# Attention over summed memory slots, then a channel mix: q turned on VectorE in 32x32 blocks of bf16 pairs, scores in 32x32 array tiles, steps in a new order

## The chip, the cores and the metric

The kernel runs on one core of a Trainium2 chip. The metric is the device time of one execution in microseconds (us). Five engines run side by side, each with its own instruction queue worked off in order: PE (TensorE: matmuls; PEld is its weight load), DVE (VectorE), ACT (ScalarE), POOL (GpSimd), SP (SyncE, which here issues DMAs). PE, DVE and ACT compute; the 16 DMA engines move data between HBM and the on-chip memory SBUF. Matmuls write PSUM, eight banks, which DVE and ACT read.

## The reference

Eight batches, eight heads, 576 tokens, 64 dims, 32 memory slots; then a channel mix over the 8 x 576 = 4608 tokens of 512 channels with a hidden width of 1024:

```python
a = exp(phi - max_s phi); a = a / sum_s a            # phi: [B, H, 576, 32]
k_m = einsum('bhsm,bhsd->bhmd', a, k)                # 32 x 64 for each head
v_m = einsum('bhsm,bhsd->bhmd', a, v)
attn = softmax_m(q @ k_m^T / 8)                      # [B, H, 576, 32]
x = attn @ v_m                                       # heads side by side: [B, 576, 512]
x_prev = x shifted by one token, zeros first
xk = mu_k * x + (1 - mu_k) * x_prev;  xr = mu_r * x + (1 - mu_r) * x_prev
out = sigmoid(xr @ w_r) * (relu(xk @ w_k) ** 2 @ w_v)
```

## The kernel before, in words

All loads cast to bf16 on their way in. Rows are read as `(a p j)`: four groups a, 128 partitions p, nine tokens j in each partition. So group a holds two heads, the even one in partitions 0 to 63 and the odd one in 64 to 127, and 64 partitions hold one head's 576 tokens as nine blocks of 64 (QR = 64). Inside the kernel a batch's tokens stand in an order of its own (JT: even j first, then odd j), cut in two halves of 320 and 256 tokens; the stores put them back.

For each batch b the function `attention(b)` offers steps by name, and the list PLAN at the head of the file says in which order they are recorded. Every engine works its own instructions off in that order, so PLAN is the schedule of all queues: `b:step` is a step of batch b, `p:` a load of the start, `c`n`:`i the hidden columns i of token chunk n, `g:`t the gate and `o:`t the output of token tile t (128 tokens, 36 of them).

The steps of a batch, in the order of its data:

- `load` (L291): four DMAs of POOL (phi, k, v, q of batch b+2), 576 KB each.
- `exp` (L224) on ACT; `z` (L243), nine matmuls that sum it, and a reciprocal on DVE; `kv` or `k`, `v` (L227), 72 matmuls each.
- `nk` (L268), `tk` (L295): k_m normalised on DVE, turned by PE, copied to `kmT` by DVE.
- `q0`, `q1` (L332), in batch 0 `qh0`, `qh1` (L319): q is turned to dims x tokens by 18 PE transposes for each, into PSUM, and copied to `qT` by DVE (in batches 0 and 1 half of it by ACT). In batches 5, 6 and 7 `qx` (L313) does it instead, with two DMA transposes that SP issues. `hold` (L263) is a small POOL copy of batch 5's `qT`, behind which the loads of the last two batches stand.
- `s0`, `s1` (L347): the scores of the even and of the odd heads, eight matmuls each in 64x32 tiles of the array (64 dims deep, 32 slots wide), then two exponentials on ACT.
- `l0` to `l3` (L365), `r0z` and its like, `w0` and its like: the softmax's sum by a matmul, its logarithm and reciprocal on ACT, the product on DVE (in batches 0 and 1 by halves, `h0z`, `y0`).
- `x0`, `x1` (L392), `dd` (L406), `k0d`, `r0d` and their like (L417): attn @ v_m, the difference to the token before, and xk and xr, by ACT and DVE. In batches 0 and 1 `mk`, `mr` (L437) do this in matmuls instead: for each half a first set of eight for the tokens themselves and one more set for each run of tokens before them, then four copies out of PSUM, two on ACT and two on DVE.

The channel mix is `c`n (`key`, L514: four matmuls, ReLU on ACT, square on DVE), `g` (`gate`, L537: four matmuls, exponential on ACT, and at every odd tile the two activations over 1024 columns that finish the sigmoid of two tiles) and `o` (`value`, L554: eight matmuls, product on DVE, `store`). `store` (L496) issues one DMA for each block of 64 tokens that a tile touches. All PSUM tiles come from one pool of eight banks in turn. `busy4` (L191) is four matmuls on zeros while batch 0's softmax runs.

Of the kernel before, what the change touches and what calls it, by code (L numbers as in the profile page):

```python
# [11 lines left out]
BF16 = mybir.dt.bfloat16  # L12
AF = mybir.ActivationFunctionType
# [5 lines left out]
    "p:q:0a 0:exp1 0:exp0 0:z 0:k0c p:q:0b 0:hn0 0:qh0 0:ht0 0:qh1 p:k:0b 0:s0 0:mub p:v:0a 0:l0 0:k1c 0:l1 0:hn1",  # L19
    "p:v:0b 0:mu 0:ht1 p:wr:0-4 0:h1z 0:v0c 0:s1 0:v1c p:phi:1 0:h0z 0:y1 0:l2 0:l3 0:nk0 0:y0 0:nk1 0:h3z 0:nr1",  # L20
    "p:wk:4-8 0:h2z 0:busy4 0:nr0 0:y3 0:y2 0:mr1 0:mr0 p:wk:0-4 0:mk1 1:exp g:2 g:0 0:mk0 g:3 1:z c0:2a c0:7b c0:6b",
    "c0:4a c0:1b p:k:1 p:q:1 c0:2b 1:k 1:nk c0:0b c0:7a c0:5b c0:3a c0:1a 1:q0 c0:3b 1:q1 1:tk c0:4b c0:0a 1:s0 p:v:1",
    "1:s1 1:v c0:6a 1:l1 1:nr1 1:l0 c0:5a p:wv:0-2 1:nk0 1:l2 p:wv:2-4 1:nk1 1:nr0 1:h1z 1:l3 0:load 1:y1 1:h2z 1:h0z",
    "1:h3z g:1 1:y3 o:3a o:2a 1:y2 1:y0 o:2b o:3b 1:mk1 o:1b 1:mk0 1:mr0 c1:5 1:mr1 c1:2 2:exp c1:6 c1:3 c1:1 c1:0",
    "1:load 2:z g:4 g:5 2:q1 2:q0 2:kv 2:nk o:0b 2:load o:1a 2:tk 3:exp 2:nv c1:7 2:s1 2:s0 c1:4 2:l2 o:0a 2:l1 3:z",
    "2:l0 2:r0z 2:w0 2:l3 2:r1z 2:w1 o:4 o:5 2:x0 3:kv 3:nk 3:nv g:6 3:tk 3:q0 3:q1 2:x1 2:dd 2:k0d g:7 g:8 3:s0",
    "2:k2d 3:s1 o:6 o:7 3:l0 2:r2d 3:l2 3:load 3:l1 2:r0d 3:l3 3:r1z c2:3 4:exp c2:2 c2:5 3:r0z 3:w1 c2:0 3:w0 c2:4",
    "c2:6 g:10 c2:1 4:z 3:x1 4:kv 4:nk 4:nv c2:7 3:x0 g:11 3:dd 4:q0 4:q1 4:tk 5:exp o:11 g:9 5:qx o:10 5:z 5:kv",
    "3:k0d 4:s1 3:k2d 4:s0 o:9 g:12 4:l3 5:nk 3:r0d 4:l2 c3:2 c3:6 5:nv 4:l0 4:l1 4:r1z 4:w1 c3:3 4:r0z 4:w0 5:tk",
    "c3:7 c3:4 3:r2d c3:0 c3:5 5:s0 5:hold 5:load 4:x1 o:8 c3:1 5:l1 4:x0 4:dd g:13 4:k2d 5:l0 g:14 o:13 4:load o:12",  # L30
    "7:exp 5:r0z 4:k0d g:16 5:w0 g:15 7:z 7:kv 5:s1 c4:5 7:qx c4:1 c4:4 6:qx 4:r0d 7:nv c4:0 c4:3 6:exp 5:l2 7:nk",
    "5:l3 c4:6 c4:2 c4:7 5:r1z 5:w1 4:r2d g:17 o:15 o:16 7:tk 5:x0 o:17 6:z 5:x1 6:kv 6:nk 7:s0 6:nv g:18 6:tk 5:dd",
    "5:k0d g:19 5:k2d o:18 o:14 6:s0 6:s1 c5:6 c5:0 6:l3 5:r0d 6:l2 6:l0 6:l1 c5:2 c5:5 6:r0z c5:7 c5:3 6:r1z 6:w1",
    "7:l0 6:w0 c5:1 g:20 7:l1 c5:4 7:s1 6:x1 5:r2d o:19 7:r0z 6:x0 6:dd 6:k2d 7:l3 g:22 6:k0d 7:w0 g:21 7:l2 g:23",
    "7:r1z o:20 o:21 7:w1 o:23 6:r2d c6:0 c6:6 c6:4 g:26 c6:1 c6:5 7:x1 c6:3 6:r0d c6:2 c6:7 7:x0 7:dd o:22 g:24 g:27",
    "7:k2d 7:k0d g:25 o:25 o:26 7:r2d o:24 c7:5 g:30 c8:6 c7:0 c7:2 c7:1 c8:1 o:27 c8:4 c7:7 6:load 7:r0d c7:3 c7:6",
    "c7:4 c8:2 c8:7 g:28 g:29 c8:3 c8:0 c8:5 g:31 o:28 o:29 o:31 7:load g:32 o:30 g:33 g:34 g:35 o:32 o:33 o:34 o:35",
]

LOADS = {None: ("phi", "k", "v", "q"), 2: ("phi", "k", "q", "v")}  # L40
# [4 lines left out]
NJ = 9  # L45
JT = (0, 2, 4, 6, 8, 1, 3, 5, 7)
# [3 lines left out]
def kernel(  # L50
# [24 lines left out]
    HALVES = (slice(0, 5 * QR), slice(5 * QR, S))  # L75
# [135 lines left out]
    def attention(b):  # L211
# [51 lines left out]
        def hold():  # L263

            spare = work.tile([1, 2], BF16, name="spare", tag="spare", bufs=1)
            nc.gpsimd.tensor_copy(spare, st["qT"][0:1, :, 0, 0])

        def norm_k(cs=(0, 1)):  # L268

            def go():  # L270
                if "kbd" not in st:
                    st["kbd"] = work.tile([128, 2, 2, D], BF16, name="kbd", tag="kbd", bufs=3)
                for c in cs:
                    nc.vector.tensor_scalar_mul(
                        st["kbd"][:, c], st["k"][c].unsqueeze(1).to_broadcast([128, 2, D]), st["rz"][:, c:c + 1])
            return go
# [18 lines left out]
        def tr_k(cs=(0, 1)):  # L295

            def go():
                n = len(cs)
                ps = ps_tile([128, n, 128], BF16, "ktps")
                for i, c in enumerate(cs):  # L300
                    nc.tensor.matmul(ps[:, i], lhsT=st["kbd"][:, c].rearrange("p h d -> p (h d)"), rhs=identity,
                                     is_transpose=True, start=True, stop=True, skip_group_check=True)
                if "kmT" not in st:
                    st["kmT"] = work.tile([128, 2, 128], BF16, name="kmT", tag="kmT", bufs=3)
                nc.vector.tensor_copy(st["kmT"][:, cs[0]:cs[0] + n], ps)
            return go

        def q_tile():
            if "qT" not in st:
                st["qT"] = work.tile([128, 2, HH * NJ // 2, QR], BF16, name="qT", tag="qT", bufs=3)  # L310
            return st["qT"]

        def cross_q():  # L313
            for hg in range(2):
                nc.sync.dma_start_transpose(out=q_tile()[:, hg],
                                            in_=qs[b % 2][ROWS[hg]].rearrange("p n d -> p (n d)"))

        def tr_q_rows(hg):

            def go():  # L320
                r = ROWS[hg]
                for i in range(2):
                    ps = ps_tile([128, NJ, QR], BF16, "qtps")
                    for n in range(NJ):
                        n0 = 2 * (NJ * i + n)
                        nc.tensor.matmul(ps[:, n], rhs=identity[r, r], is_transpose=True,  # L326
                                         lhsT=qs[b % 2][r, n0:n0 + 2, :].rearrange("p n d -> p (n d)"),
                                         start=True, stop=True, skip_group_check=True)
                    (nc.scalar.copy if i else nc.vector.tensor_copy)(q_tile()[:, hg, NJ * i:NJ * (i + 1)], ps)
            return go  # L330

        def tr_q(i):  # L332
            def go():
                pss = [ps_tile([128, NJ, QR], BF16, "qtps") for _ in range(2)]
                for n in range(NJ):
                    n0 = 2 * (NJ * i + n)
                    for hg in range(2):
                        r = ROWS[hg]
                        nc.tensor.matmul(pss[hg][:, n], rhs=identity[r, r], is_transpose=True,  # L339
                                         lhsT=qs[b % 2][r, n0:n0 + 2, :].rearrange("p n d -> p (n d)"),  # L340
                                         start=True, stop=True, skip_group_check=True)
                for hg in range(2):
                    (nc.scalar.copy if b < 2 and hg else nc.vector.tensor_copy)(
                        q_tile()[:, hg, NJ * i:NJ * (i + 1)], pss[hg])
            return go

        def scores(c):  # L347

            def go():
                if "e" not in st:  # L350
                    st["e"] = work.tile([128, 2, S], BF16, name="e", tag="e", bufs=3)
                pss = [half_tile(hf, "scps") for hf in range(2)]
                for g in (0, 2, 1, 3):
                    m = slice(g * M, (g + 1) * M)
                    for hf in range(2):
                        n = [NJ * g + j for j in JT[5 * hf:5 + 4 * hf]]
                        r = ROWS[n[0] % 2]
                        nc.tensor.matmul(pss[hf][m, :], lhsT=st["kmT"][r, c, m],  # L358
                                         rhs=st["qT"][r, c, n[0] // 2:n[-1] // 2 + 1].rearrange("p j t -> p (j t)"),
                                         start=True, stop=True, skip_group_check=True)  # L360
                for hf in range(2):
                    nc.scalar.activation(st["e"][:, c, HALVES[hf]], pss[hf], AF.Exp, scale=scale)  # L362
# [41 lines left out]
        before = [[(QR, 5 * QR, 5 * QR), (1, QR, 4 * QR)], [(5 * QR, S, 0)]]  # L404

        def diff(pr, n=1):  # L406

            def go():
# [3 lines left out]
                for lo, hi, p0 in before[1] + before[0]:  # L412
                    nc.vector.tensor_sub(d[:, :, lo:hi], x[:, :, lo:hi], x[:, :, p0:p0 + hi - lo])  # L413
# [23 lines left out]
        def mixed(w, hf):  # L437

            def go():
# [7 lines left out]
                for i in range(ND):  # L447
# [6 lines left out]
                 "z": esum, "nk": norm_k(), "nv": norm_v, "tk": tr_k(), "load": reload, "mu": load_mu, "mub": load_mu_b, "qx": cross_q,  # L454
                 "zr": sum_rows, "hold": hold}
        for i in range(2):
            steps[f"q{i}"] = tr_q(i)
            steps[f"qh{i}"] = tr_q_rows(i)
# [16 lines left out]
        for i in range(2):  # L475
            steps[f"s{i}"] = scores(i)
# [19 lines left out]
    def store(o, t, cols):  # L496
        g = t * 128
        eng = nc.sync
        while g < (t + 1) * 128:
            b, r = divmod(g, S)  # L500
            p = g - t * 128
            j, p0 = divmod(r, QR)
            n = min(QR - p0, (t + 1) * 128 - g)
# [117 lines left out]
```

## Time and profile before

| | us |
|---|---|
| median of 3 runs (lowest, highest) | 209.13 (207.54, 209.47) |
| the profiled execution | 208.79 |
| span of its instructions | 207.0 |
| PE busy, DVE busy, ACT busy in it | 192.7, 133.9, 159.4 |
| first matmul, last matmul's product | 5.93, 203.23 |
| software DMA queue (the loads) | 20.91 MB |

The profile gives, for one execution, the busy time of each engine, the chain of work that ended last, and the groups of equal instructions. The span starts with the first instruction; 1.8 us of the execution's time lie around it. A "start to start" time below is the distance between the first instruction of a piece of work on PE and the first of the next piece: since matmuls are pipelined, it is what the piece costs PE, and the busy time of a row is more.

### The profile page before, as it was taken

The numbers are of one execution on the slowest core, as the hardware profiler recorded it, in microseconds if no ns is written. First come the engines' busy times: TensorE is split into PE (matmuls) and PEld (weight loads), VectorE is DVE, ScalarE is ACT, GpSimd is POOL, SyncE is SP. The second block draws the span as 40 slices with busy tenths as digits, with TensorE's granted clock in tenths as the row PEclk, the third lists the DMA queues.
The fourth block names the chain that finished last, engine by engine and source line by source line (L and its number), as shares of the span: only waits on it lengthen the run. The fifth ranks groups of instructions, "written<-read, shape, count | busy, mean of one in ns | idle before, by whom it ended". The sixth has DMA issues, their size and how long they took to land.

```text
span 207.0 us, 5511 instructions
## 1 busy us (share of the span) xinstructions
PE 192.7 (93%) x2213; PEld 103.6 (50%) x2235; DVE 133.9 (65%) x360; ACT 159.4 (77%) x314; POOL 29.6 (14%) x46
## 2 busy tenths in 40 slices
PE   0489999999999999999999999999999999999992
PEld 0355577745655445544458654444444444444441
DVE  1236455884668996899594969767887856615232
ACT  3246999987968998979899977899968655686570
POOL 7644222201504000007400000000000000000000
PEclk9999999999999999999999999999999999999999
DMA  6999999999999999298999997832060215202525
GB/s 160 178 208 260 207 207 205 261 221 292 209 284 240 262 269 201 61 133 205 187 231 298 198 165 115 189 71 52 0 152 5 51 33 119 54 0 62 135 67 141
DMA packets 31641, 33.06 MB, mean 160 GB/s; under 512 B 9072, under 2 KB 26752, under 8 KB 31616
## 3 DMA queue, kind: packets, MB, share of 16 engines
q0 software_dynamic: 17392, 20.91, 54.2%
q1 hardware_dynamic: 13456, 10.96, 24.5%
q10 hardware_dynamic: 768, 0.85, 1.3%
q8 instruction: 17, 0.28, 0.5%
q14 instruction: 8, 0.07, 0.1%
HBM read 38.28 MB, written 9.44 MB: 231 GB/s over the span
## 4 chain that ended last, share of the span: by engine, by line
PE 89%; DMA 6%; issue 1%; POOL 1%; ACT 1%; DVE 0%; SPq 0%; POOLq 0%; DVEq 0%
PE pk L520 31%; PE pv L565 29%; PE pr L543 15%; DMA q<-in_q_dram 4%; PE kvps L237 3%; PE zps L372 2%; PE mxps L288 2%; DMA qT<-q 2%; PE scps L358 2%; PE nops L288 2%; PE qtps L339 1%; PE idle L195 1%; PE zps L247 1%; PE mub L200 1%; PE qtps L326 1%
## 5 line engine op out<-in xcount | busy, mean ns | idle before, releaser
L520 PE MATMUL pk<-xkT,wk 128*128 128x512 bf16 (+4 forms) x346 | 66.9, 340 | 0.4
L565 PE MATMUL pv<-wv,sq 128*128 128x512 bf16 (+1 forms) x322 | 65.6, 353 | 0.4
L524 ACT ACTIVATE rl<-pk 128x512 bf16<-128x512 f32 (+3 forms) x80 | 41.9, 560 | 9.9 <-PE pk L520 8.7
L528 DVE TENSOR_TENSOR sq<-rl 128x512 bf16<-128x512 bf16 (+5 forms) x104 | 32.3, 340 | 26.0 <-ACT rl L524 25.0
L565 PEld LDWEIGHTS <-sq 128*128 128x128 bf16 x328 | 31.4, 98 | 30.0 <-issue 0.5
L520 PEld LDWEIGHTS <-wk 128*128 128x128 bf16 x352 | 32.9, 98 | 26.5 <-issue 0.5
L567 DVE TENSOR_TENSOR o<-sg,pv 128x512 f32<-128x512 f32 (+1 forms) x41 | 24.9, 619 | 18.9 <-PE pv L565 14.1
L543 PE MATMUL pr<-wr,xrT 128*128 128x512 bf16 x134 | 34.6, 381 | 0.5
L548 ACT ACTIVATE sg<-pr 128x512 f32<-128x512 f32 x36 | 21.3, 611 | 12.3 <-PE pr L543 5.2
L543 PEld LDWEIGHTS <-xrT 128*128 128x128 bf16 x144 | 13.5, 98 | 15.4 <-ACT xrT L449 0.4
L550 ACT ACTIVATE sg<-sg 128x1024 f32<-128x1024 f32 x18 | 19.0, 1057 | 0.6
L551 ACT ACTIVATE sg<-sg 128x1024 f32<-128x1024 f32 x18 | 19.0, 1057 | 0.6
L401 ACT CAST x<-nops 128x320 bf16<-128x320 f32 (+1 forms) x48 | 15.8, 428 | 3.6 <-PE nops L288 3.6
L423 DVE TENSOR_SCALAR mu_d<-diff,mu 128x576 bf16<-128x576 bf16 x48 | 15.5, 364 | 0.1
L389 DVE TENSOR_TENSOR atn<-e,lz 128x576 bf16<-128x576 bf16 (+2 forms) x20 | 12.4, 635 | 4.0 <-ACT lz L382 3.8
L377 ACT ACTIVATE lz<-zps 128x320 f32<-128x320 f32 (+1 forms) x32 | 11.9, 420 | 1.6 <-PE zps L372 1.6
L362 ACT ACTIVATE e<-scps 128x320 bf16<-128x320 f32 (+1 forms) x32 | 11.0, 416 | 1.5 <-PE scps L358 1.5
L382 ACT ACTIVATE lz<-lz 128x576 f32<-128x576 f32 (+2 forms) x20 | 11.6, 600 | 0.2
L413 DVE TENSOR_TENSOR diff<-x 128x1024 bf16<-128x1024 bf16 (+1 forms) x18 | 9.0, 554 | 3.4 <-ACT x L401 3.4
L225 ACT ACTIVATE em<-ph 128x1152 bf16<-128x1152 f32 (+1 forms) x9 | 9.4, 1050 | 2.1 <-DMA ph<-in_phi_dram 2.1
L237 PE MATMUL kvps<-kv,em 64*32 64x128 bf16 (+1 forms) x720 | 9.3, 219 | 1.0 <-DMA kv<-in_k_dram 1.0
L424 DVE TENSOR_TENSOR xkT<-x,mu_d 128x1152 bf16<-128x1152 bf16 x12 | 9.1, 759 | 0.4
(66 smaller groups left out, 140.7 us busy)
## 6 DMA issues: line engine op xcount, KB each, us to landing
out_dram<-o SPq DMA_DIRECT2D x61, 128.0 KB, 2.4
ph<-in_phi_dram POOLq DMA_DIRECT2D x7, 576.0 KB, 20.8
kv<-in_k_dram POOLq DMA_DIRECT2D x7, 576.0 KB, 17.3
q<-in_q_dram POOLq DMA_DIRECT2D x7, 576.0 KB, 21.3
kv<-in_v_dram POOLq DMA_DIRECT2D x7, 576.0 KB, 18.8
out_dram<-o SPq DMA_DIRECT2D x18, 64.0 KB, 5.6
wk<-in_moe_w_k_dram POOLq DMA_DIRECT2D x2, 512.0 KB, 14.7
wv<-in_moe_w_v_dram POOLq DMA_DIRECT2D x2, 512.0 KB, 20.0
```

Source lines behind the costliest of these rows:

```text
L237: nc.tensor.matmul(kvps[c][g * M:(g + 1) * M], lhsT=em[ROWS[c], j, g, :], rhs=kv5[ROWS[c], parts, g, j, :], start=j == 0, stop=j == NJ - 1 ...
L401: nc.scalar.copy(st["x"][:, i, sl], pss[i])
L423: nc.vector.tensor_scalar_mul(t[:, i], st["d"][:, pr + i, :], mu1[:, o:o + 1])
L520: nc.tensor.matmul(pk[:, p0 - lo:p1 - lo], lhsT=wk_sb[:, di, fi * 128:(fi + 1) * 128], rhs=xk_T[:, di, p0 % RING:p0 % RING + p1 - p0], sta ...
L524: nc.scalar.activation(rl, pk, AF.Relu)
L528: nc.vector.tensor_mul(sq[:, fi, p:p + p1 - p0], rl[:, p0 - lo:p1 - lo], rl[:, p0 - lo:p1 - lo])
L543: nc.tensor.matmul(pr, lhsT=xr_T[:, di, c0:c0 + 128], rhs=wr_sb[:, di, :], start=(di == 0), stop=(di == ND - 1))
L548: nc.scalar.activation(sg[:, t % 2], pr, AF.Exp, scale=-1.0)
L550: nc.scalar.activation(sg, sg, AF.Ln, bias=1.0)
L551: nc.scalar.activation(sg, sg, AF.Exp, scale=-1.0)
L565: nc.tensor.matmul(pv[:, cols], lhsT=sq[:, fi, p:p + 128], rhs=wv_sb[:, fi, cols], start=(fi == 0), stop=(fi == NF - 1))
L567: nc.vector.tensor_mul(o[:, cols], gated[t // 2][:, t % 2, cols], pv[:, cols])
```

## The change

- q is turned by DVE alone: `turn_q` views the bf16 pairs of q as 32-bit words and transposes them in 32x32 blocks. A block of 32 tokens by 64 dims comes out as 32 dim pairs by 32 tokens, the two dims of a pair side by side. The PE transposes, the copies, the DMA transposes (`qx`) and `hold` are gone.
- The scores follow that layout: 32 dims at a time, first the even and then the odd ones, accumulated in PSUM; 16 matmuls of 288 tokens for `s0` or `s1`, and from batch 1 on one step `s` of 32 with four PSUM tiles. `rhs` takes every second bf16 of `qT`. `kbd` and `kmT` are laid out for it (`nk`, `tk`).
- Tokens stand in two halves of 288, each nine blocks of 32 (PB). `mk`, `mr` of the second half take four sets instead of two; `dd` is two subtractions over both halves at once, one of a single token and the copy of the first token (four instructions, as before). A store covers up to four blocks in one DMA (two in the last two tiles).
- `settle`: the two activations that finish a gate are a step of their own (`sg`).
- `busy4` is gone; batch 2 loads v before q; PLAN is another order throughout. The matmuls, loads and element counts of all other steps are as they were.

```diff
-    "p:q:0a 0:exp1 0:exp0 0:z 0:k0c p:q:0b 0:hn0 0:qh0 0:ht0 0:qh1 p:k:0b 0:s0 0:mub p:v:0a 0:l0 0:k1c 0:l1 0:hn1",
-    "p:v:0b 0:mu 0:ht1 p:wr:0-4 0:h1z 0:v0c 0:s1 0:v1c p:phi:1 0:h0z 0:y1 0:l2 0:l3 0:nk0 0:y0 0:nk1 0:h3z 0:nr1",
-    "p:wk:4-8 0:h2z 0:busy4 0:nr0 0:y3 0:y2 0:mr1 0:mr0 p:wk:0-4 0:mk1 1:exp g:2 g:0 0:mk0 g:3 1:z c0:2a c0:7b c0:6b",
...
+    "p:q:0a 0:exp0 0:exp1 0:z 0:mub 0:k0c p:k:0b 0:qh0 0:k1c 0:hn0 0:ht0 0:s0 p:q:0b 0:hn1 0:l0 0:h0z 0:qh1 0:ht1",
+    "0:y0 p:v:0b 0:v1c 0:l1 0:nr1 p:v:0a 0:s1 p:wr:0-4 0:nk1 0:v0c 0:nr0 0:h1z 0:l2 0:h2z 0:nk0 p:wk:4-8 0:y1 0:mu",
+    "0:y2 0:l3 0:h3z 0:y3 p:phi:1 0:mk0 0:mr1 0:mr0 0:mk1 g:2 c0:6a c0:7a 1:exp p:wk:0-4 c0:5b g:3 c0:2a g:1 c0:0a",
...
-LOADS = {None: ("phi", "k", "v", "q"), 2: ("phi", "k", "q", "v")}
+LOADS = {None: ("phi", "k", "v", "q")}
...
-    HALVES = (slice(0, 5 * QR), slice(5 * QR, S))
+    HS = S // 2
+    PB = 32
+    HALVES = (slice(0, HS), slice(HS, S))
...
+        def turn_q(rows_, gs):
+            def go():
+                dst = q_tile()[rows_, gs].rearrange("p g n h -> p (g n h)")
+                src = qs[b % 2][rows_, gs.start * NJ:gs.stop * NJ].rearrange("p n d -> p (n d)")
+                nc.vector.transpose(dst.bitcast(U32), src.bitcast(U32))
+            return go
...
-                pss = [half_tile(hf, "scps") for hf in range(2)]
-                for g in (0, 2, 1, 3):
+                pss = {(c, hf): half_tile(hf, "scps") for c in cs for hf in range(2)}
+                for h in range(2):
+                    for g in range(HH):
+                        m = slice(g * M, (g + 1) * M)
+                        for c in cs:
+                            for hf in range(2):
+                                r = slice((2 * c + hf) * PB, (2 * c + hf + 1) * PB)
+                                nc.tensor.matmul(pss[c, hf][m, :], lhsT=st["kmT"][r, h, m], rhs=st["qT"][r, g, :, h],
+                                                 start=h == 0, stop=h == 1, skip_group_check=True)
...
-        before = [[(QR, 5 * QR, 5 * QR), (1, QR, 4 * QR)], [(5 * QR, S, 0)]]
+        before = [[(PB, HS, 0), (1, PB, HS - PB)], [(HS + PB, S, HS), (HS + 1, HS + PB, S - PB), (HS, HS + 1, HS - 1)]]
...
-            steps[f"q{i}"] = tr_q(i)
-            steps[f"qh{i}"] = tr_q_rows(i)
+            steps[f"q{i}"] = turn_q(slice(0, 128), slice(2 * i, 2 * i + 2))
+            steps[f"qh{i}"] = turn_q(ROWS[i], slice(0, HH))
...
-            j, p0 = divmod(r, QR)
-            n = min(QR - p0, (t + 1) * 128 - g)
-            dst = out[b].rearrange("(p j) d -> p j d", j=NJ)[p0:p0 + n, JT[j], cols]
-            eng.dma_start(out=dst, in_=o[p:p + n, cols])
+            hf, r = divmod(r, HS)
+            j = r // PB
+            n = min(NJ - j, ((t + 1) * 128 - g) // PB, 2 if t >= NTOK // 128 - 2 else 4)
+            dst = out[b].rearrange("(h p j) d -> h j p d", h=2, j=NJ)[hf, j:j + n, :, cols]
+            eng.dma_start(out=dst, in_=o[p:p + n * PB, cols])
...
-            if t % 2 == 1:
-                nc.scalar.activation(sg, sg, AF.Ln, bias=1.0)
-                nc.scalar.activation(sg, sg, AF.Exp, scale=-1.0)
+    def settle(p):
+        def go():
+            nc.scalar.activation(gated[p], gated[p], AF.Ln, bias=1.0)
+            nc.scalar.activation(gated[p], gated[p], AF.Exp, scale=-1.0)
+        return go
```

## The prediction

> **What bounds the kernel now.** I read the page's busy shares first, then the chain, then one window for the body, then the waits. From the page:
>
> ```profile
> PE 192.7 (93%) x2213; PEld 103.6 (50%) x2235; DVE 133.9 (65%) x360; ACT 159.4 (77%) x314; POOL 29.6 (14%) x46
> ...
> DMA  6999999999999999298999997832060215202525
> ...
> PE 89%; DMA 6%; issue 1%; POOL 1%; ACT 1%; DVE 0%; SPq 0%; POOLq 0%; DVEq 0%
> ```
>
> From the first softmaxes on, PE is the bound, as the window from the first `mixed` matmul to the last product shows (columns: PE, PEld, DVE, ACT, POOL busy):
>
> ```profile
> 19.11:203.20 184.09, 182.36 (x1996) 97.05 (x2017) 126.92 (x331) 151.28 (x297) 18.15 (x25) 1.00 0.79 156
> ```
>
> PE idles 1.7 us in 184.1. The one data wait of that stretch in PE's list of waits is batch 6's q, turned by DMA:
>
> ```profile
> PE scps L358 <- DMA qT<-q: 0.4, 1, 0.4
> ```
>
> The DMA row says something else: until slice 16 (83 us) it stands at 9. The loads run without a pause; in 20 to 40 us:
>
> ```profile
> DMA  9999999999999999999999999999999999999999
> ...
> q0 software_dynamic: 4693, 4.33, 126.0%
> ...
> ```
>
> 4.33 MB in 20 us is 0.217 MB/us, so a load that casts (576 KB, 0.59 MB) takes 2.7 us, and phi, which is read at the width it keeps, about half, 1.4. Asked window by window, the loads' queue has moved 13.75 MB by 71 us and 16.17 by 84; added up in the order of the loads, q of batch 4 ends at 13.83 MB, 71 us, ahead of its use at 81.2, and q of batch 5 at 16.19 MB, 84 us. Batch 1's q lands at 30.5 (a POOL load waits for its slot till then) and is used at 31.2. So loads are just ahead of PE, and nothing but spare room on the DMA engines keeps them there.
>
> **The change part by part.** Sums are against the profiled execution, 208.79 (span 207.0, 1.8 around it); the median of the three runs is 209.13, 0.3 above.
>
> *The turn of q, PE.* A turn's start to start on PE is read from the timeline (start, us):
>
> ```profile
> 50.79 0.70 PE L339 MATMUL qtps<-identity,q 64*128 64x64 bf16 x36
> 51.42 0.80 PE L237 MATMUL kvps<-kv,em 64*32 64x128 bf16 x72
> ...
> 54.98 0.46 PE L358 MATMUL scps<-qT,kmT 64*32 64x320 bf16 x16
> 55.38 1.04 PE L520 MATMUL pk<-xkT,wk 128*128 128x512 bf16 x4
> ```
>
> 0.63 for a batch; batches 2 to 4 three times that, batch 1 0.37 twice: 2.63 us leave PE. Batch 6's wait for the DMA turn goes too, 0.45. What is late next there is the turn on DVE.
>
> *The turn of q, DVE.* No row shows this operation. 576 four-byte words a partition: below lies the 450 ns of the copy of 576 bf16 (L343), above twice a 512-word float product (L567, 684 ns), 1.37 us. Nearest is one pass at the product's rate, 684 x 576/512 = 0.77. Fourteen of these (batch 0: two of 1.4) replace fourteen copies of 0.45: DVE goes from 126.9 to some 131 us of 184, so it stays under PE. Batch 0's two turns stand in the chain of the start; there `k0b` takes q's landing slot (11.0) and q's second half k's (12.7). Turn to 14.1, scores at 15.0 (before 15.7), first `mixed` matmul at 18.2 (before 19.1); the 16 PSUM tiles of its four steps, emptied by two engines at 0.44 each, push the first gate to 21.4 (21.34 before), with 0.48 of `mixed` already done. I take -0.4; between -1.2 and +1.0. `mub` and `busy4` lay in waits and cost nothing either way.
>
> *Scores.* Sixteen matmuls for both heads' parity cost 0.40 (above), eight cost 0.28 (108.46 to 108.74): a second round of eight tiles adds 0.12. The new step has 32 in two rounds of 16 tiles. If all 16 run together, 0.40; if eight do, as the rows show, 0.28 + 3 x 0.12 = 0.64; if every second element also halves the rate, 1.1. I take 0.45, nearest to the two rounds, since 72 kvps matmuls in 0.73 us show 10 ns from one to the next, 0.32 for 32. Today's seven batches cost about 3.2 (two are split in 0.28 + 0.28): 7 x 0.45 = 3.15, no change; -0.4 to +4.5.
>
> The Trainium skill, "TensorE: Matmul & The Clock Gate", section "Wait — 56ns, not 53.3ns?", says that starts never come closer than some 25 ns; by it the 32 would take 0.8 and the seven batches 2.4 us more. The kvps row (10 ns) speaks against it.
>
> *`mixed`.* Sixteen matmuls take 0.36 (40.70 to 41.06) and 24 take 0.47, so a set of eight short ones 0.12; batch 1 has four sets more, +0.44; batch 0's are in the start. New waits of the new order: +0.5 (0 to 3). ACT, `nk`, `dd` and `settle` keep their element counts beside PE's 182 us of work. POOL loses `hold`, so the last eight loads are issued when their buffers are free, some 8 us earlier; SP loses six DMA turns.
>
> PE's side: -2.63 - 0.45 - 0.4 + 0.44 + 0.5 = -2.5.
>
> *The stores.* This is the part that decides. SP and ACT issue 57 stores for 82, with 2 KB rows as before, but their shape is new: 64 rows on both sides before; now 128, 96 or 64 partitions on one side and [4, 32], [3, 32] or [2, 32] rows on the other. From the list of DMA issues:
>
> ```profile
> out_dram<-o SPq DMA_DIRECT2D x61, 128.0 KB, 2.4
> ...
> mu<-in_moe_mu_k_dram SPq DMA_DIRECT2D x1, 2.0 KB
> ```
>
> The second row, four rows on both sides, has no landing time. The trace's completion records say why: a 64-row store raises its semaphore in 16 steps, one for each engine, the four small loads in five each, one at the issue and four as data lands. So an outer dimension of four is dealt to four engines. The new stores lie between these rows. I take the smaller count (4, 3, 2), as a deal has to cut both sides. With 16, the stores cost nothing new.
>
> The Trainium skill, "DMA: Bandwidth & Descriptors", section "Why a DMA increments its semaphore by 16 and not by 1", states the same for both sides: the largest number up to 16 that divides both outer dimensions, on the lowest-numbered engines. Only the small loads show it here.
>
> If always the same engines are taken, the first two carry 2.79 MB of stores each, where each carries 0.59 now. An engine's rate, from the end of the run, where stores alone run:
>
> ```profile
> GB/s 304 140 257 70 281 117 305 351 398 375 258 375 316 152 187 176 234 258 293 316 258 223 47 0 0 0 0 0 0 0 0 0 0 0 0 0 0 0 0 0
> ```
>
> 398/16 = 24.9 GB/s, so 64 KB, which every store of two to four blocks puts on the first engine, take 2.6 us, half tiles 1.3, and a tile with 2 + 2 blocks 5.3. A load has a share on that engine and lands when it is through. Landing without stores, from 38.4 (end of wv) on in steps of 2.7 and 1.4: q2 47.9, q3 57.4, q4 66.9, v5 73.7, phi6 87.3. Stores that PE's order puts ahead come on top; PE's own times are the sum of its pieces in the new order:
> - scores of batch 2: q2 47.9 + eight half stores 10.5 + turn 1.5 = 59.9; PE is there at 53. +6.9.
> - scores of batch 3: 57.4 + 18.4 + 1.5 = 77.3 against 65.1 + 6.9. +5.3.
> - `4:q0`: 66.9 + 23.8 = 90.7 against 73 + 12.2 on DVE: 5.5, in which the squares queue behind the turn, then ACT's ReLU (three buffers), then PE (eight banks). PE feels 3.5.
> - `5:kv`: 73.7 + 31.7 = 105.4 against 86.5 + 15.7. +3.2.
> - v7 and phi6 for `7:kv` and `6:exp`: 129.5 for the later against 102.5 + 18.9, 8 us of ACT's wait with gates and exponentials behind it; +6.
> Together 25. The end: the last four tiles put 16 us on the first engine, which starts 3.6 before PE's end and ends 12.4 after it; today the last packets end 1.7 after. +10.7.
>
> Sum: 208.8 - 2.5 + 25 + 10.7 = 242. Waiting stores also hold the four output buffers (more), and stalled PE delays stores and so frees loads (less); I take 240.
>
> **The rivals.**
> 1. *All 16 engines serve a store* (the partition side decides). Then only PE's side is left: 206.3. For it: today's 64-row stores land in 2.4. Against: the five-step completions. Point where it decides: at eight engines a store puts 32 KB on each, less than half the load, and the loads' slack covers it.
> 2. *Few engines, but loads are not held up* (the engine favours them, or other engines are taken in turn): only the end and the output buffers cost, 208.8 - 2.5 + 10.7 = 217. Against: from 54 to 72 us, with stores beside them, loads moved 3.56 MB where their pace alone would give 3.9.
> 3. *The score tiles run one after another*, eight at a time and at half rate: 1.1 a batch, +4.5 on whichever case holds; 211 with rival 1, and above 0.8 a batch that one is no gain.
>
> **How the numbers follow.** Forecast, few engines and loads held up: 0.62, own range 222 to 254 (half the load waits; or output buffers add as much again as their excess). Rival 1: 0.17, 204 to 208.5. Rival 2: 0.18, 212 to 222. Rival 3 with 16 engines: 0.03, 209 to 213. The range 212 to 254 leaves out rival 1 and the third, 0.20. Faster by over 1% (below 206.7; about what a measurement of this kernel can tell from no change): rival 1's better part, 0.11; within 1%: its other part, 0.06; slower: the rest, 0.83.
>
> **What would show it.** Right: landings of stores of 5 us and more where 2.4 stood; waits of DVE's turn and of PE's kvps on q, k, v DMAs between 50 and 130 us; at least 10 us of DMA after the last matmul; DMA's mean share low while loads are late; DVE turns near 0.77, `scps` 32 in 0.45, no `qtps`. Wrong: stores landing in 2 to 3 us with PE busy through.

## The result and the profile after

The changed kernel takes 248.07 us (median of 6, 246.15 to 248.97), the kernel before 208.57 beside it on the same chip: ratio 1.188, 95% interval 1.182 to 1.194. The forecast was 240, range 212 to 254. The profiled execution of after is 248.97 (span 247.2).

First the page: engines' busy time, the slices, the chain ("..." stands for lines left out).

```profile
PE 196.6 (80%) x2223; PEld 103.2 (42%) x2245; DVE 139.9 (57%) x360; ACT 157.0 (64%) x310; POOL 29.3 (12%) x45
...
PE   0589999999039999599447999999999999999000
...
PEclk9999999999756999999975999999999999999755
DMA  7999999999989352299962221220321031123210
...
PE 54%; DMA 21%; issue 12%; ACT 2%; DVE 2%; POOL 2%; POOLq 0%; DVEq 0%
```

PE is no longer busy throughout: it has three dips (from 62, from 99 and from 117 us, at 6.18 us a slice) and three empty slices at the end. Behind the first and the last dip its granted clock falls, and from 80 to 105 us DMA's mean share stands at 2 to 5 though loads are still to come. The chain that ended last has 21% of DMA where it had 6%.

The window from the first `mixed` matmul to the last product (columns: PE, PEld, DVE, ACT, POOL busy; clock, DMA share, GB/s), against 184.1 us with 182.4 of PE before:

```profile
17.88:229.38 211.50, 188.54 (x2023) 98.96 (x2044) 131.56 (x332) 150.21 (x296) 18.73 (x25) 0.94 0.60 128
```

PE idles 23.0 us in it (1.7 before). The waits of PE name three kinds of releaser (total us, times, longest us):

```profile
PE kvps L240 <- DVE o L550: 8.6, 2, 5.7
...
PE zps L348 <- ACT e L338: 5.6, 4, 4.6
PE nops L288 <- DVE o L550: 3.9, 1, 3.9
PE kvps L240 <- DMA kv<-in_v_dram: 3.0, 1, 3.0
```

8.6 + 3.9 = 12.5 us go to DVE's product `o`. DVE's timeline shows what it stood for, and PE's what followed:

```profile
67.25 0.69 DVE L550 TENSOR_TENSOR o<-sg,pv 128x512 f32<-128x512 f32 x1 [5.69 <-issue]
72.27 0.69 DVE L550 TENSOR_TENSOR o<-sg,pv 128x512 f32<-128x512 f32 x1 [4.33 <-DMA out_dram<-o]
...
103.40 0.69 DVE L550 TENSOR_TENSOR o<-sg,pv 128x512 f32<-128x512 f32 x1 [3.21 <-DMA out_dram<-o]
```

```profile
67.99 1.16 PE L240 MATMUL kvps<-kv,em 64*32 64x128 bf16 x71 [5.69 <-DVE o L550]
73.01 0.54 PE L288 MATMUL nops<-atn,vb 32*64 32x288 bf16 x8 [3.86 <-DVE o L550]
...
77.08 2.56 PE L548 MATMUL pv<-wv,sq 128*128 128x512 bf16 x8
79.57 0.48 PE L334 MATMUL scps<-qT,kmT 32*32 32x288 bf16 x32
```

The product needs one of four output buffers, and the stores of the tiles before have not landed. The trace's completion records (the steps in which each DMA raises its semaphore) show it for all three, the first too, which carries no name: the stores issued at 44.24, 49.79 and 80.49 have their last completions at 67.17, 72.09 and 103.27, 22 to 23 us after their issue, and the products start 0.1 to 0.2 us later. PE stands behind them for want of a bank. Eight `pv` matmuls that take 1.89 us elsewhere then take 2.56: the granted clock is 0.50 from 64.8 to 78.4.

The other rows belong in the main to batches 6 and 7: PE waits 3.0 us for batch 7's v, and 4.6 of the 5.6 us of `zps` for an exponential of the scores that stands on ACT behind batch 6's phi. ACT waits 11 us for that phi. The load was issued late, because POOL works in order and batch 7's k, ahead of it, waits for batch 5's `kvps`:

```profile
129.51 1.16 ACT L228 ACTIVATE em<-ph 128x1152 bf16<-128x1152 f32 x1 [11.15 <-DMA ph<-in_phi_dram]
```

```profile
105.29 0.74 POOL L110 DMA_DIRECT2D kv<-in_k_dram  x1 [19.17 <-PE kvps L240]
...
110.07 0.76 POOL L106 DMA_DIRECT2D ph<-in_phi_dram  x1
```

It also took 19.4 us to land. Twelve of its 16 completions are in by 118.69, 0.3 us after ACT begins to wait; the last four come between 118.73 and 129.49. With batch 7's v it is the same: twelve by 114.19, the last at 121.57, just ahead of PE's next matmul at 121.70. So what PE and ACT waited for here is a few engines on which these loads ran late.

The stores, from the list of issues and from the bandwidth of the last 13.2 us (40 slices):

```profile
out_dram<-o SPq DMA_DIRECT2D x19, 256.0 KB
```

```profile
GB/s 68 87 74 81 81 74 68 50 50 50 53 47 56 53 43 50 56 50 43 53 47 50 47 50 50 47 47 50 50 47 47 47 25 22 25 19 0 0 0 0
```

A store of four blocks has no landing time in this list, since it has fewer than 16 completions: one at the issue and four more. The 57 stores leave 347 completions in all, which is five for each of the 25 with four blocks, four for the nine with three, three for the 14 with two, and 16 for the nine with one. The end runs for 8 us at 50 GB/s and for 1.3 at 25: two engines, then one, of 25 each. The last product ends at 229.38, the span at 247.2: 17.8 us, where it was 3.4 before (the last product there starts at 203.23 and ends at 203.65).

The change does to q and the scores what it says: no `qtps` is left, DVE's turns take 768 ns, 1375 for the two halves, and 32 score matmuls 0.42 us from start to start (54.56 to 54.98).

### The profile page after: what moved, and what is told of

Its sections match the earlier page's. It is cut to its first block, busy times and chain, and to the rows that moved or that the text cites. A ratio compares the mean times of both kernels' runs of the same rounds, so it can differ in the third digit from the quotient of the medians.

```text
span 247.2 us, 5493 instructions
## 1 busy us (share of the span) xinstructions
PE 196.6 (80%) x2223; PEld 103.2 (42%) x2245; DVE 139.9 (57%) x360; ACT 157.0 (64%) x310; POOL 29.3 (12%) x45
## 4 chain that ended last, share of the span: by engine, by line
PE 54%; DMA 21%; issue 12%; ACT 2%; DVE 2%; POOL 2%; POOLq 0%; DVEq 0%
PE pk L499 20%; PE pv L548 17%; DMA kv<-in_k_dram 10%; PE pr L522 9%; DMA ph<-in_phi_dram 8%; DMA out_dram<-o 3%; PE kvps L240 2%; PE mxps L288 2%; PE zps L348 2%; PE scps L334 1%; ACT e L338 1%; DVE o L550 1%; PE nops L288 1%; DVE xkT L427 1%; PE ktps L301 1%
## 5 line engine op out<-in xcount | busy, mean ns | idle before, releaser
L548 PE MATMUL pv<-wv,sq 128*128 128x512 bf16 (+1 forms) x320 | 67.2, 357 | 0.4
L503 ACT ACTIVATE rl<-pk 128x512 bf16<-128x512 f32 (+2 forms) x80 | 42.5, 565 | 15.9 <-PE pk L499 14.9
L522 PE MATMUL pr<-wr,xrT 128*128 128x512 bf16 x135 | 40.7, 426 | 1.0 <-issue 0.4
L527 ACT ACTIVATE sg<-pr 128x512 f32<-128x512 f32 x36 | 21.4, 601 | 15.0 <-PE pr L522 13.3
L377 ACT CAST x<-nops 128x288 bf16<-128x288 f32 x48 | 15.7, 424 | 11.9 <-PE nops L288 11.9
L319 DVE STREAM_TRANSPOSE qT<-q 128x576 uint32<-128x576 uint32 (+1 forms) x16 | 13.2, 838 | 8.4 <-DMA q<-in_q_dram 8.4
L338 ACT ACTIVATE e<-scps 128x288 bf16<-128x288 f32 x32 | 10.6, 416 | 7.5 <-PE scps L334 7.4
L240 PEld LDWEIGHTS <-em 64*32 64x32 bf16 x720 | 7.7, 99 | 18.0 <-issue 17.7
L365 DVE TENSOR_TENSOR atn<-e,lz 128x576 bf16<-128x576 bf16 (+1 forms) x20 | 12.5, 632 | 2.9 <-ACT lz L358 2.9
L353 ACT ACTIVATE lz<-zps 128x288 f32<-128x288 f32 x32 | 12.0, 419 | 1.3 <-PE zps L348 1.2
L348 PE MATMUL zps<-e,sumh 128*128 128x288 bf16 x32 | 7.7, 320 | 5.6 <-ACT e L338 5.6
```

The costliest lines, as they stand in the source:

```text
L240: nc.tensor.matmul(kvps[c][g * M:(g + 1) * M], lhsT=em[ROWS[c], j, g, :], rhs=kv5[ROWS[c], parts, g, j, :], start=j == 0, stop=j == NJ - 1 ...
L377: nc.scalar.copy(st["x"][:, i, sl], pss[i])
L503: nc.scalar.activation(rl, pk, AF.Relu)
L522: nc.tensor.matmul(pr, lhsT=xr_T[:, di, c0:c0 + 128], rhs=wr_sb[:, di, :], start=(di == 0), stop=(di == ND - 1))
L527: nc.scalar.activation(sg[:, t % 2], pr, AF.Exp, scale=-1.0)
L548: nc.tensor.matmul(pv[:, cols], lhsT=sq[:, fi, p:p + 128], rhs=wv_sb[:, fi, cols], start=(fi == 0), stop=(fi == NF - 1))
```

## The experiments

### One store for each block

```diff
-            n = min(NJ - j, ((t + 1) * 128 - g) // PB, 2 if t >= NTOK // 128 - 2 else 4)
+            n = 1
```

> The changed kernel with one store for each block of 32 rows (155 + stores in all for 57), everything else as changed. Few engines (the theory on record): each store has 32 rows on both sides, so all 16 engines serve it, the waits on buffers and loads go, no kvps or turn waits in 50 to 130 us, and the time is what the sum gave for the other parts, 206.3, plus 1 to 2 for eight small stores at the end: 206 to 209. Rival, the turn on DVE, the score tiles or the new order make it slow: 240 or more.

Measured: 212.76 us, ratio to before 1.015 (1.007 to 1.023). All of the rest of the change stays, and 35.3 of the 39.5 us are gone. The page:

```profile
PE 192.5 (91%) x2245; PEld 101.5 (48%) x2245; DVE 139.6 (66%) x360; ACT 156.7 (74%) x310; POOL 29.4 (14%) x45
...
PEclk9999999999999999999978999999999999999996
DMA  6999999999999999499995211320321015011343
...
out_dram<-o SPq DMA_DIRECT2D x121, 64.0 KB, 1.7
```

Three times the DMAs, and landings of 1.7 us; each of the 164 stores has 16 completions. So the shape of the stores decides, not q's turn or the scores. But 212.8 is above the 206 to 209 that the theory gave. One stall, at 105 to 112 us (PE idle for 3.0, then at half the clock), is left:

```profile
106.78 1.16 ACT L228 ACTIVATE em<-ph 128x1152 bf16<-128x1152 f32 x1 [4.75 <-DMA ph<-in_phi_dram]
```

It is batch 6's phi again, issued behind the same wait, without any store on few engines: part of the time is the new order's own. Of the load's 16 completions 15 are in by 103.50 and the last comes at 106.76; what held that one engine is not shown.

### The kernel before, with its stores in pairs

```diff
+            if j + 1 < NJ and JT[j + 1] == JT[j] + 2 and g + 2 * QR <= (t + 1) * 128:
+                n = 2 * QR
+                dst = out[b].rearrange("(p j) d -> j p d", j=NJ)[JT[j]:JT[j] + 3:2, :, cols]
```

> The kernel before, with the two 64-row blocks of a tile in one store where their rows lie two apart (28 of 36 tiles): the new shape of stores alone, nothing else of the change. Few engines: 28 tiles put 128 KB each on the same two engines, 3.7 MB or 149 us at 24.9 GB/s beside 97 us of loads, so at least 246, with the end 260 (245 to 290). Rival: 208 to 210, as the bytes are the same and the stores fewer.

Measured: 274.03 us in one run, 65 over the kernel before. Fewer DMAs, in 28 of 36 tiles of twice the size and with an outer dimension of two on the DRAM side, and nothing else changed. DVE's largest wait on a DMA is the buffers' again, and PE waits for loads too:

```profile
DVE o L570 <- DMA out_dram<-o: 30.6, 5, 19.4
...
PE pk L523 <- DVE o L570: 18.8, 2, 17.1
...
PE kvps L237 <- DMA kv<-in_v_dram: 9.5, 2, 7.9
```

The rival, that 128 partitions on the other side keep all 16 engines, falls by 64 us.

### The last four tiles alone by blocks

```diff
-            n = min(NJ - j, ((t + 1) * 128 - g) // PB, 2 if t >= NTOK // 128 - 2 else 4)
+            n = min(NJ - j, ((t + 1) * 128 - g) // PB, 1 if t >= NTOK // 128 - 4 else 4)
```

> The changed kernel with the stores of the last four tiles by single blocks of 32 rows (all engines by the theory). Few engines: only the end shrinks, from 18 us behind the last matmul to 5 to 8, 237 (234 to 240). If the end is not made by the engines: 246 to 249.

Measured: 235.76 us, one run; span 234.0 against 247.2. The last product ends at 229.1, as in after, and the end behind it falls from 17.8 to 4.9. The end and the body are two separate costs, and the merged stores of the last four tiles make 13 us of the end.

### Seven output buffers

```diff
-                outs[t] = work.tile([128, Dm], F32, name="o", tag="o", bufs=4)
+                outs[t] = work.tile([128, Dm], F32, name="o", tag="o", bufs=7)
```

(`qT` has two buffers instead of three, to make room.)

> The changed kernel with seven output buffers for four (and two of qT for three, to make room). If DVE's waits for output buffers hold PE between 60 and 80 us, as the profile after suggests: they go, 236 (232 to 241). If late loads hold it, as the prediction had it: DVE's waits go, but the same loads end when they did, so 244 to 249.

Measured: 241.01 us, one run: 7 us less than after. DVE's waits for `out_dram` fall to 1.0 us (8.5 in after, with the unnamed 5.7 beside it), and those for q grow from 8.4 to 18.1; DVE's list of waits has none for the two `qT` buffers. So loads appear in the stores' place:

```profile
65.59 1.44 DVE L319 STREAM_TRANSPOSE qT<-q 128x576 uint32<-128x576 uint32 x2 [2.75 <-DMA q<-in_q_dram]
```

```profile
DVE qT L319 <- DMA q<-in_q_dram: 18.1, 6, 8.9
...
PE kvps L240 <- DMA kv<-in_v_dram: 5.9, 2, 3.8
PE zps L348 <- ACT e L338: 5.7, 4, 4.8
...
PE scps L334 <- DVE kmT L306: 2.9, 2, 2.6
```

Neither theory holds alone; 241.0 is the upper edge of what the buffers by themselves were to give. The buffers are the first to bind; once they don't, the loads do, by shorter waits than the forecast gave them. Batch 3's q lands at 65.6, 8 us behind the 57.4 worked out without stores, and not 18.4.

### What is left of the new order: the loads of batches 6 and 7

Two kernels on top of the first one (one store for each block). In the first, the load steps change places; in the second, the last four tiles' stores also alternate between SP and ACT.

```diff
-... 5:tk 5:load sg:6 4:load c3:7 ...
+... 5:tk 4:load sg:6 5:load c3:7 ...
```

> The changed kernel with one store for each 32-row block, and the load steps of batches 6 and 7 in the other order (4:load ahead of 5:load), so that batch 6's phi no longer stands behind batch 7's k, which waits on POOL's queue until batch 5's kvps matmuls are through. Theory: what kept the one-block kernel at 212.8 and not at 206 to 209 is this one hold-up (4.75 us of ACT before the exponential of batch 6's phi, then PE at a lower clock), so it falls to 207 to 209, and the stretch from 100 to 120 us shows PE busy throughout. Rival: the loss is spread over the new order, or the hold-up moves to batch 7's loads: 211 to 214.

> As the kernel with the swapped loads, and the 32-row stores of the last four tiles dealt alternately to SP and ACT instead of 16 on SP in a row. Theory: after the last product the one-block kernel spends 6.0 us on issuing stores, some 0.65 us each on one queue, so half of the issues on the other queue takes 1.5 to 2.5 us off: 205 to 207, and the end is 3.5 to 4.5 us after the last product. Rival: the end is set by the landing of the last stores, whatever queue issues them, or ACT's issues delay its last activations: within 0.5 us of the kernel with the swapped loads.

Measured: 214.97 (ratio 1.035, 1.031 to 1.039) and 214.76 (1.032, 1.030 to 1.035). Both misses. The swap is 2 us worse: phi of batch 6 is on time, but batch 6's k, v and q now stand ahead of batch 7's, which are used first:

```profile
106.09 1.16 PE L240 MATMUL kvps<-kv,em 64*32 64x128 bf16 x72 [4.34 <-DMA kv<-in_v_dram]
```

The rival was right in kind: the hold-up moves to batch 7 (215.0 lies above its 211 to 214). The second kernel's 0.2 us is within the spread: with eight small stores behind the last product, a second queue alone doesn't shorten the end.

### Only batch 6's phi early, then q of batch 7 later

```diff
-LOADS = {None: ("phi", "k", "v", "q")}
+LOADS = {None: ("phi", "k", "v", "q"), 7: ("phi", "phi6", "k", "v", "q"), 6: ("k", "v", "q")}
```

and, for the second kernel,

```diff
-... 7:z 7:kv 7:q0 6:exp 5:s 7:nv g:14 7:q1 4:dd g:15 4:k0d 4:k2d ...
+... 7:z 7:kv 6:exp 5:s 7:nv g:14 4:dd g:15 4:k0d 4:k2d 7:q0 7:q1 ...
```

> The changed kernel with one store for each 32-row block, in its own order, but with batch 6's phi alone (1.4 us of loads) issued ahead of batch 7's k; batch 6's k, v and q stay behind batch 7's. Theory: the swap of whole batches moved the hold-up to batch 7's v because it put 9.5 us of transfers ahead of it in a queue that has only 5 to 7 us idle; phi alone fits into that idle time, so ACT's 4.75 us before batch 6's exponential goes and nothing takes its place but part of batch 7's q (1.9 us on DVE): 207 to 210. Rival: what PE waits for around 104 us is batch 7's q on DVE, as late as before, and the phi was only the last of two: 211 to 213.

> As the kernel with batch 6's phi early, and DVE's two turns of batch 7's q recorded behind batch 4's xk copies instead of ahead of the differences of batch 4. Theory: no engine is left waiting for a load between 95 and 115 us, PE's busy share of 100 to 120 us is that of the other stretches, and the time is that of PE's side with the end as it is: 206.5 to 208.5. Rival: the turn was not what the other engines waited for: the same as the kernel with the early phi.

Measured: 210.17 (ratio 1.004, 1.001 to 1.007) and 208.88 (1.000, 0.998 to 1.002); before 208.73. The first edit takes 2.6 us off the 212.76 (each beside its own runs of the kernel before, which differ by 0.1), the second 1.3 more; both lie just above their ranges (207 to 210, and 206.5 to 208.5). In the second kernel PE has no stall left from 100 to 120 us; first the kernel with one store for each block, then this one:

```profile
100.00:120.00 20.00, 16.69 (x205) 9.34 (x205) 13.48 (x36) 13.48 (x27) 0.00 (x0) 0.91 0.84 183
```

```profile
100.00:120.00 20.00, 19.70 (x284) 12.13 (x282) 16.44 (x43) 18.32 (x37) 0.00 (x0) 1.00 0.85 172
```

and its last product:

```profile
201.38 0.42 DVE L550 TENSOR_TENSOR o<-sg,pv 128x256 f32<-128x256 f32 x1 [0.45 <-PE pv L548]
```

So the new order's own cost was some 3.9 us (the four runs with one store for each block spread from 210.2 to 213.3): one load behind another's wait on POOL's queue, and DVE's turn waiting for a load with other work queued behind. The last product ends at 201.80 (203.65 before), but 5.6 us of end follow instead of 3.4.

### The end: one last tile, two or three queues

```diff
-            if t >= NTOK // 128 - 2:
-                eng = nc.scalar
+            if t >= NTOK // 128 - 4:
+                eng = nc.scalar if eng is nc.sync else nc.sync
...
-    mixes["o"] = {str(t): value(t) if t < NT - 1 else value(t, ((0, 1), (1, 2)), 2) for t in range(NT)}
+    mixes["o"] = {str(t): value(t) for t in range(NT)}
```

The second kernel takes SP, ACT and POOL in turn.

> As the kernel with the early phi and the late turns, and at the end: the stores of the last four tiles alternate between SP and ACT, and the last tile is one product over 512 columns with four stores of 64 KB instead of two products over 256 columns with eight of 32 KB. Theory: what is left over PE's side is the issue of many small stores behind the last product (5.6 us from its end to the end of the span, 3.4 in the kernel before); four issues on two queues instead of eight take 1.0 to 1.5 us off, of which the longer last product (684 instead of 420 ns) takes 0.3 back: 207.5 to 208.3, at or just below the kernel before. Rival: the landing of the last store sets the end and the issues lie beside it: 208.5 to 209.2.

> As the kernel with the whole last tile, with the stores of the last four tiles dealt to SP, ACT and POOL in turn. Theory: fewer issues in a row on each queue, 0.3 to 0.7 us less: 207 to 207.8. Rival: POOL's DMAs take longer from issue to landing than those of SP and ACT, so the last of them ends later: 208 to 210.

Measured: 207.21 us (ratio 0.994, 0.992 to 0.997) and 207.81 (0.996, 0.994 to 0.999); before 208.65. Both lie a little below the kernel before, the first by 1.4 us, the second by 0.8. The last product of the first:

```profile
200.60 0.69 DVE L550 TENSOR_TENSOR o<-sg,pv 128x512 f32<-128x512 f32 x1 [1.04 <-PE pv L548]
```

It ends at 201.29, and the span at 205.4: 4.1 us of end. Half as many stores behind the last product, on two queues, shorten the end by 1.5 us, where two queues alone did nothing. The third queue was to give 0.3 to 0.7 us and costs 0.6; POOL's stores land in 2.9 us where ACT's take 2.1.

## Why the prediction was right, point by point

The mechanism that it said decides, decides: a store whose outer dimension is 4, 3 or 2 runs on as many engines, and loads that share these engines land late. The sum came out 7 us low by errors of both signs, so that it is this close is in part luck. Against the profiled execution before it is +40.2 us in all, of which the table leaves 0.7 open, with PE's own work taken from the repaired kernel (the last but one above, 207.21):

| step | predicted | measured |
|---|---|---|
| PE's side without waits | -2.5 | -2.6 |
| waits of PE in the body | +25, all on loads | +21: 12.5 on output buffers, 8.6 in the main on loads |
| lower clock behind the waits | not in the sum | +6.6 |
| the end | +10.7 | +14.5 |
| sum | +33, of which +31 was taken | +39.5 |

- *PE's side.* Right. In the repaired kernel the last product ends 2.36 before that of the kernel before, though it is itself 0.27 longer. The first `mixed` matmul starts at 17.88 (18.2 predicted), the first gate at 21.04 (21.4). DVE's turn: 768 and 1375 ns against 770 and 1400. The 32 score matmuls: 0.42 against 0.45. The rule on 25 ns between starts, quoted in the prediction, would make that 0.8, so the row decides against it in this case; the rival of serial tiles falls with it.
- *The stores' engines.* Right: the first two experiments settle it from both sides, the completions count the engines, and the end shows two at 50 GB/s, one at 25. The Trainium skill, "DMA: Bandwidth & Descriptors", section "Why a DMA increments its semaphore by 16 and not by 1", states the count (the largest number up to 16 that divides both outer dimensions), and these shapes agree: 32 rows on both sides land in 1.7 us.
- *"A load ... lands when it is through".* Right in kind. The records give the last of a load's 16 completions, and the twelfth, by which the 12 engines that serve no merged store should be done (the records don't name engines):

| load | after: twelfth, last | one store a block: twelfth, last | last, predicted |
|---|---|---|---|
| q of batch 3 | 59.19, 64.76 | 60.32, 61.21 | 75.8 |
| q of batch 4 | 69.11, 80.14 | 72.66, 73.51 | 90.7 |
| v of batch 5 | 78.50, 93.61 | 80.87, 82.28 | 105.4 |
| v of batch 7 | 114.19, 121.57 | 98.45, 101.23 | |
| phi of batch 6 | 118.69, 129.49 | 103.27, 106.76 | 129.5 |

The bytes hide this: by 80 us the loads' queue had moved 15.56 MB, against 15.57 before, since the other engines had run ahead.
- *"Stores that PE's order puts ahead come on top".* This was too much: it set a load behind all stores issued earlier. Batch 2's scores ran at 54.56, predicted 59.9, with no load wait, and the first three loads of the table landed some 11 us sooner than predicted. On the shared engines loads and stores went by turns. From 67 to 99 us the merged stores have their last completions at 67.17, 72.09, 76.64, 81.89, 87.67, 93.41 and 99.20, and after each of these one load has its own, at 71.03, 75.58, 80.14, 82.16, 87.85, 93.61 and 99.38. So the stores waited as well, up to 26 us from issue to landing (5.8 for one issued at 151, when the loads were over), and by 80 us SP's queue had moved 1.06 MB against 2.11 with one store for each block. So the output buffers bound first (12.5 us), which the text named with no number; the loads came next (the seven buffers).
- *v7 and phi6, +6.* The size was near (3.0 + 5.6, not all of it phi6's), and the engines the cause, as said; but that phi6 landed at 129.49 as predicted is chance. The sum had it at 87.3 without stores, and it was issued at 110.07 (93.74 with one store for each block), since it stood behind batch 7's k on POOL's queue. That wait holds it up in a lighter form without any merged store: "New waits of the new order: +0.5 (0 to 3)" should have been some 3.9. The order of POOL's loads was in the text of PLAN, and its waits were not walked through.
- *The clock.* Missed. PE's busy time in the window is 188.5 us, against 181.9 in the repaired kernel with the same matmuls: 6.6 us. The trace grants 0.50 around waits of PE of 5.7 and 3.9 us, of 3.0 (at 121.7) and of 4.6 (at 131.0), and full clock behind one of 2.95 (at 104.1). With seven buffers it fell around waits of 2.6 and 2.1 us too, and with the last four tiles by blocks it stayed full behind one of 3.0 (at 121.2), so the length of the wait alone does not decide. The Trainium skill, "TensorE: Matmul & The Clock Gate", "Part 1: The HAM clock gate", says that the clock halves after an idle window of some 3.4 us and returns after as much busy time. The stretches at 0.50 fit such a window (13.6, 3.4 and 6.8 us, multiples of 3.4), but the waits of 2.1 to 3.0 us around which it fell are shorter than the idle window that the page asks for.
- *The end.* Right in kind, 4 short. It counted the stores of the last four tiles on the first engine, from 3.6 us before PE's end on (225.8). Stores of tiles whose products end at 219.4 and 221.0 go ahead of them on the same engines and land up to 228.41; that these make up most of the 4 us is worked out, not tested.

## What to carry to other kernels

Before stores are merged to save issues, read the outer dimension on both sides of the DMA: 57 merged stores cost 35 us against 164 small ones. When a transfer gets slower, walk first through the buffers that it holds, then through what shares its engines, and look there at the last completions of a load, not at the bytes of its queue. Count the matmul clock behind every wait of 2 us or more: in these runs some of 2.1 to 3.0 us lowered it and some did not. Where loads are issued in order, a load that waits for its buffer holds up all behind it; one 1.4 us load moved ahead of such a wait was worth 2.6 us.

## What was not expected of the hardware

- On the engines that loads and merged stores share, both were late, by turns of one store and one load, while the other engines ran ahead: of the load of batch 5's q, twelve completions were in by 81.40 and the last four came between 93.03 and 99.38.
- PE's granted clock stood at 0.50 for 13.6 us in one piece (64.8 to 78.4), in which PE was busy for 6.3 us; two waits of PE, 5.7 and 3.9 us, lie in or just ahead of it.
- The number of stores behind the last product counted more than the queues they were on: eight of 32 KB ended 5.6 us after it, with six of them on ACT (the kernel with q of batch 7 later) as with four (the one with the loads swapped and two queues), and four of 64 KB on two queues 4.1 us.
